# Moving a state-space branch behind the exponentials of an attention loop: one loop from the first rows instead of four stages

## The chip, the cores and the metric

The kernel runs on one core of one Trainium2 chip. The metric is device time in microseconds (us) of that core: the median of the fast runs. In the profile, PE is TensorE (PEld its weight loads), DVE is VectorE, ACT is ScalarE, POOL is GpSimd, SP the engine that issues most transfers. L519 is line 519 of the kernel of that run. The program lists each engine's instructions in a fixed order, with semaphores to wait at. In the traces below, what is listed behind a waiting instruction waits with it: in r8, a VectorE copy out of PSUM whose input was ready began only after the reductions listed before it, the first of which had waited 10.01 us.

## The reference, cut to what matters

```python
x = A_x                                                  # 1 x 2048 x 512, bf16
g = sigmoid((x * gate_w).sum(-1, keepdims=True))
# a: softmax attention, 32 heads of 16, then @ wo
qkv = (x @ wqkv)...; p = softmax(q k^T * 16**-0.5); a = (p v) @ wo
# b: a diagonal state-space model as a long convolution, 512 channels x 128 complex modes
dt = exp(log_dt); K[d,l] = Re sum_n C*exp(dt*A*l)*dt*B
b = causal_conv(x, K) + x * Dskip
return g * a + (1 - g) * b
```

Per head and query row there are 2048 exponentials: 32 x 2048 x 2048 in all, which is 1024 instructions of 128 partitions x 1024 elements on ScalarE. No other engine computes them here.

## The kernel before

It has two blocks with a barrier between them. Block 1 loads, projects (storing Q and K to device memory) and builds powers of the state matrix for 128 time steps with Exp and Sin on ScalarE. Block 2 is the attention loop, with the chunk scan on VectorE and the convolution's matmuls on TensorE placed between the steps, and a closing combine.

```python
# block 1, ScalarE: the tables (64 Exp, 128 Sin of 128x1024)
actc.inc(a.activation(TE[:, u % 8, :], pa_slots[v_re(u) % 2], AF.Exp))          # L435
...
a.activation(TSn[:, u % 2, :], src, AF.Sin)                                      # L442
actc.inc(a.activation(TCs[:, u % 2, :], src, AF.Sin, scale=-1.0, bias=HPI))      # L443
... (cut: projections, products, transfers of the tables through device memory)
# block 2, ScalarE: the softmax exponentials
for c in range(NCHUNK):                                                          # 1024
    a.wait_ge(stc.sem, c + 1)
    ...
    exc.inc(a.activation(ET[:, c % NRCH, 0:QW * n], chunk_src(c)[:, 0:QW * n], AF.Exp, scale=DH ** -0.5))  # L775
# block 2, TensorE
for sx in range(NSTEP):                       # 512 steps of two exponentials
    st_step(sx + LAS)                         # scores, 4 matmuls in 4 row groups    L894
    pv_step(sx)                               # probabilities x V, 4 column groups   L922
    for d in ysched[...]: y_channel(d)        # convolution output, 3 matmuls a channel
# after the loop, VectorE, 16 times
cv2(v.tensor_tensor(fb1, xr, Dbc, ALU.mult)); ... (cut: L872 to L875, gate and add)
```

The softmax here doesn't subtract the row's maximum and nothing guards it: scores larger than these inputs give would overflow.

## Time and profile before

| stretch (us) | what runs | ACT busy | granted clock |
|---|---|---|---|
| 0 to 166 | loads, parameters, projections | 18.6 of 166 | 0.97 |
| 166 to 542 | state-space tables | 203.8 of 376 | 0.50 |
| 542 to 1504 | attention loop | 941.0 of 962 | 0.50 |
| 1504 to 1573 | combine | 0 of 69 | 0.52 |

Median time 1577.24 us (1575.1 to 1579.39, 4 runs).

From the page of the kernel before: busy time of the engines, then busy tenths in 40 slices of the span (a 9 is 90% or more; PEclk is the granted TensorE clock in tenths).

```profile
PE 994.5 (63%) x8332; PEld 294.0 (19%) x8340; DVE 732.8 (47%) x1678; ACT 1163.4 (74%) x1249; POOL 170.6 (11%) x201
...
PE   0199555655653166666566666567888768888744
...
ACT  0100666666662299999899999899999989999920
...
PEclk9999555555555555555555555555555555555555
```

The row ACT shows the stages: nothing, 60%, a gap, then nearly full from slice 14 on, and nothing at the end. The table above is from the view of engine times in four stretches (span, busy time and count for each engine, clock, DMA share, GB/s):

```profile
0.00:166.00 166.00, 86.49 (x347) 34.27 (x354) 118.57 (x194) 18.58 (x23) 1.08 (x9) 0.97 0.42 99
166.00:542.00 376.00, 189.54 (x2296) 82.44 (x2296) 120.56 (x290) 203.83 (x201) 116.53 (x132) 0.50 0.90 193
542.00:1504.00 962.00, 689.88 (x5632) 170.36 (x5628) 434.33 (x1087) 940.95 (x1026) 52.96 (x60) 0.50 0.26 60
1504.00:1573.00 69.00, 28.55 (x62) 6.95 (x64) 59.37 (x108) 0.00 (x0) 0.00 (x0) 0.52 0.19 57
```

And the costliest groups: busy us and mean ns of one, then the idle time of that engine just before them and who ended it.

```profile
L775 ACT ACTIVATE ET<-pr 128x1024 bf16<-128x1024 f32 x1024 | 939.5, 1049 | 48.4 <-PE pr L894 47.7
L922 PE MATMUL pb<-ET,VE 128*32 128x512 bf16 x2048 | 315.7, 607 | 154.5 <-ACT ET L775 154.3
```

So the third stage is bound by ScalarE (one exponential every 939.5 / 1024 = 0.917 us, starts overlapping ends), and the other three stages, 611 us, are not.

### The profile page before, as it was taken

What the parts mean: (1) busy time and instruction counts of PE and PEld (TensorE: products, weight loads), DVE (VectorE), ACT (ScalarE), POOL (GpSimd) and SP (SyncE); (2) the same over time, 40 slices, a digit from 0 to 9 for tenths busy, and PEclk for the clock granted to TensorE, in tenths of its full rate; (3) what the DMA queues carried; (4) which work ended last, traced back from release to release, by engine and by line L of the source; (5) the groups of instructions that cost most, each with busy time, mean ns of one, the idle gap of its engine ahead of it and who ended that gap; (6) DMA issues with size and microseconds to landing.
All of it is one profiled execution on the core that took longest, in us unless ns stands there. A gap on an engine that the chain in (4) does not pass through costs nothing. (4 is left out here: it accounts for less than half of the span.)

```text
span 1572.3 us, 21690 instructions
## 1 busy us (share of the span) xinstructions
PE 994.5 (63%) x8332; PEld 294.0 (19%) x8340; DVE 732.8 (47%) x1678; ACT 1163.4 (74%) x1249; POOL 170.6 (11%) x201
## 2 busy tenths in 40 slices
PE   0199555655653166666566666567888768888744
PEld 0044122222222011111111111111222222222210
DVE  7777233333333248787788782131232123123168
ACT  0100666666662299999899999899999989999920
POOL 0000233333332000000000000000111111111000
PEclk9999555555555555555555555555555555555555
DMA  6513699989999700000100000101555555555312
GB/s 150 54 67 147 137 186 198 205 199 185 206 201 201 181 14 1 1 1 1 54 1 1 1 0 1 49 5 41 121 122 125 134 145 121 128 126 123 88 31 70
DMA packets 346760, 150.21 MB, mean 96 GB/s; under 512 B 320160, under 2 KB 330272, under 8 KB 346656
## 3 DMA queue, kind: packets, MB, share of 16 engines
q1 hardware_dynamic: 331296, 98.47, 29.2%
q0 software_dynamic: 15360, 50.34, 12.9%
q8 instruction: 66, 1.08, 0.3%
q14 instruction: 38, 0.31, 0.1%
HBM read 68.03 MB, written 44.30 MB: 71 GB/s over the span
## 5 line engine op out<-in xcount | busy, mean ns | idle before, releaser
L775 ACT ACTIVATE ET<-pr 128x1024 bf16<-128x1024 f32 x1024 | 939.5, 1049 | 48.4 <-PE pr L894 47.7
L922 PE MATMUL pb<-ET,VE 128*32 128x512 bf16 x2048 | 315.7, 607 | 154.5 <-ACT ET L775 154.3
L894 PE MATMUL pr<-QK 16*128 16x512 bf16 x2048 | 313.5, 603 | 142.6 <-ACT ET L775 89.1
L847 DVE CAST OS<-pb 128x512 bf16<-128x512 f32 x32 | 22.1, 692 | 335.5 <-PE pb L922 335.5
L764 POOL DMA_DIRECT2D Tst<-gm_kp_scr x64 | 56.5, 883 | 920.9 <-PE pb L944 906.9
L397 DVE TENSOR_TENSOR PR<-TE,TCs 128x1024 bf16<-128x1024 bf16 x64 | 44.3, 692 | 237.5 <-ACT TCs L443 119.2
L442 ACT ACTIVATE TSn<-pr 128x1024 bf16<-128x1024 f32 x64 | 65.7, 1026 | 102.6 <-PE pr L488 84.1
L922 PEld LDWEIGHTS pb<-ET,VE 128*32 128x32 bf16 x2048 | 56.5, 101 | 413.1 <-ACT ET L775 411.0
L856 DVE TENSOR_SCALAR ON<-OT,Rz 128x16 bf16<-128x16 bf16 x512 | 121.8, 238 | 18.3
L519 PE MATMUL pb<-urev,Qt 128*128 128x16 bf16 x1024 | 47.2, 192 | 111.8 <-DMA Qt<-gm_pt_scr 72.8
L894 PEld LDWEIGHTS pr<-QK 16*128 16x128 bf16 x2048 | 55.4, 99 | 305.8 <-ACT ET L775 234.1
L273 POOL DMA_DIRECT2D gm_pt_scr<-PR x64 | 56.8, 888 | 371.3 <-DVE PI L398 370.0
L844 DVE CAST Ysb<-pb 128x512 bf16<-128x512 f32 x16 | 11.1, 691 | 159.7 <-PE pb L944 159.6
L435 ACT ACT_TABLE_LOAD x8 | 10.3, 1283 | 100.3 <-PE pr L488 100.3
L940 PE MATMUL pb<-urev,Tst 128*128 128x16 bf16 x512 | 69.9, 193 | 6.2 <-DVE junkb L845 6.2
L488 PE MATMUL pr<-MU,ahl 32*128 32x512 bf16 x128 | 56.1, 608 | 26.0 <-ACT TE L435 22.4
L443 ACT ACTIVATE TCs<-pr,cst 128x1024 bf16<-128x1024 f32 x64 | 71.4, 1115 | 0.0
L488 PE MATMUL pr<-MU,bhl 32*128 32x512 bf16 x128 | 65.8, 616 | 7.8 <-ACT TCs L443 5.8
L435 ACT ACTIVATE TE<-pr 128x1024 bf16<-128x1024 f32 x64 | 62.4, 1022 | 6.8 <-PE pr L488 6.4
L940 PEld LDWEIGHTS pb<-urev,Tst 128*128 128x128 bf16 x512 | 46.3, 104 | 104.2 <-issue 104.2
L944 PE MATMUL pb<-sgi,Pst 128*128 128x15 bf16 x512 | 62.5, 174 | 0.0
L943 PE MATMUL pb<-sgr,Pst 128*128 128x15 bf16 x512 | 62.2, 174 | 0.0
(144 smaller groups left out, 1069.3 us busy)
## 6 DMA issues: line engine op xcount, KB each, us to landing
Pst<-gm_pt_scr SPq DMA_DIRECT2D x64, 512.0 KB, 4.5
gm_pt_scr<-PR POOLq DMA_DIRECT2D x64, 256.0 KB, 4.8
gm_pt_scr<-PI POOLq DMA_DIRECT2D x64, 256.0 KB, 5.3
Tst<-gm_kp_scr POOLq DMA_DIRECT2D x64, 256.0 KB, 5.2
gm_qk_scr<-qkev SPq DMA_DIRECT2D x16, 512.0 KB, 2.6
QK<-gm_qk_scr SPq DMA_DIRECT2D x16, 512.0 KB, 5.6
xr<-in_A_x_dram SPq DMA_DIRECT2D x32, 128.0 KB, 2.1
x_sb<-in_A_x_dram SPq DMA_DIRECT2D x1, 2048.0 KB, 10.9
```

The source lines that it names most:

```text
L273: stq[u % 2].inc(g.dma_start(AP(pt_scr, ((8 * tt) * 2 + part) * NMODE * T, [[T, P], [2 * NMODE * T, 8], [1, T]]), srcb[:, u % 2, :]), 16)
L435: actc.inc(a.activation(TE[:, u % 8, :], pa_slots[v_re(u) % 2], AF.Exp))
L442: a.activation(TSn[:, u % 2, :], src, AF.Sin)
L443: actc.inc(a.activation(TCs[:, u % 2, :], src, AF.Sin, scale=-1.0, bias=HPI))
L488: ins = t.matmul(dstt[:, 512 * bb:512 * (bb + 1)], src[32 * t4:32 * t4 + 32, slot8, :], MU2[32 * t4:32 * t4 + 32, 512 * bprime:512 * (bpri ...
L775: exc.inc(a.activation(ET[:, c % NRCH, 0:QW * n], chunk_src(c)[:, 0:QW * n], AF.Exp, scale=DH ** -0.5))
L856: cv2(v.tensor_scalar(ON[:, c0 + 16 * w:c0 + 16 * w + 16], OT[:, c0:c0 + 16], Rz[:, 4 * i + Bh:4 * i + Bh + 1], None, ALU.mult))
L894: ins = t.matmul(st_dst(tt), QK[32 * j:32 * j + 16, w, 1, 128 * kt:128 * (kt + 1)], QK[32 * j:32 * j + 16, w, 0, QW * qc:QW * (qc + 1)], s ...
L922: ins = t.matmul(half[32 * j:32 * j + 32, :], VE[:, kt, 32 * h:32 * h + 32], ET[:, c % NRCH, QW * (tt % CT):QW * (tt % CT + 1)], start=(kt ...
L940: t.matmul(Yps[:, col:col + NCK], Tst[:, slot, cpos, :], urev[:, :, d], start=True, stop=(NCK == 1))
L943: t.matmul(Yps[:, col + 1:col + NCK], Pst[:, slot, 2 * cpos, :], sgr[:, d, 0:NCK - 1], start=False, stop=False)
L944: ins = t.matmul(Yps[:, col + 1:col + NCK], Pst[:, slot, 2 * cpos + 1, :], sgi[:, d, 0:NCK - 1], start=False, stop=True)
```

## The change

Its intent is to start the 512 attention steps as soon as the first rows and one head group are projected, and to put everything else behind them: the remaining projections, the state-space branch in chunks of 64 steps with its powers made by repeated complex multiplication on VectorE and GpSimd, the scan on GpSimd, and the combine. A small planner in Python walks through the 512 steps. At each step every engine gets a budget in microseconds; side work is a set of generators that say what they wait for and what the next piece will cost. The plan fixes the order of each engine's instructions; the chip then runs them with semaphores.

```diff
+class Sched:
+    def _ok(self, t, req):
+        ... "AFTER": a mark was set so many steps ago; "LOCK": the shared PSUM bank MB is free
+        if self.bud[k] > 0:
+            self.bud[k] -= req[1]
+            return True
+    def step(self, rate):
+        for k, r in rate.items():
+            self.bud[k] = min(self.bud[k] + r, r) if r > 0 else 0.0
+        ... each generator advances while _ok
 ... (cut: buffer placement, automatic semaphores, parameters, tables)
+    def scan():                       # 4 quarters x 31 chunks, on GpSimd
+                e = "POOL"
+                    yield (e, .65)
+                    op(e, ... v.tensor_tensor(s2, G, MU, ALU.mult))     # 128x256 fp32, three more like it
+                yield (e, .35)
+                op(e, ... v.tensor_copy(sg, G))
 ... (cut)
+    for q in range(512):
+        ex(2 * q)
+        if q + 1 < NQ:
+            qk(q + 1)
+        ex(2 * q + 1)
+        rate = dict(PE=.62 if q > 50 else 1.0, DVE=1.5, POOL=1.8)
+        pv(q - 1)                     # (with exceptions at block borders, cut)
+        if kt == 0 and b >= 1:
+            norm(b - 1)
+        if q < len(first):
+            proj(*first[q], mb)
+        sch.step(rate)
```

Nearly all of the side work on TensorE goes through one PSUM bank, MB (a few projections at the start and the last output blocks use others), which VectorE has to copy out before the next user gets it.

## The prediction

> **What bounds it now.** The page's 40 slices and the table of stretches show four stages in series. 0 to 166 us: parameter arithmetic, loads, projections (ScalarE busy 18.6 us). 166 to 542 us: state-space tables, with ScalarE's Exp and Sin, VectorE products and 90% DMA share; ScalarE busy 203.8 of 376 us. 542 to 1504 us: attention, ScalarE busy 941 of 962 us. 1504 to 1573 us: the combine on VectorE, ScalarE idle. So the attention stage is bound by the exponentials: 1024 of 128x1024, one every 0.915 us (group of costliest instructions: 939.5 us busy, plus 48.4 us idle, of which about 20 us lie inside the stage: three reloads of Q and K and the start). In that stage TensorE is 690 of 962 us busy at a granted clock of 0.50, waiting mostly for ET; VectorE is under half busy. About 610 us run outside the ScalarE-bound stage.
>
> **What the change does.** It leaves the number and shape of exponentials, 1024 of 128x1024, so the floor is 1024 x 0.917 = 939 us. All ScalarE state-space work (128 Sin, 64 Exp, 200 us) is gone: powers come from VectorE and GpSimd multiplications. Projections, tables, scan and the closing combine become side work put behind the attention steps (two exponentials, 1.83 us each step).
>
> Does it fit in 512 steps (about 940 us)?
> - TensorE: two groups of four 512-column matmuls take 0.61 us each (timeline), 1.2 us per step, leaving 0.6. Side work, estimated from traced rates (0.38 to 0.41 us per 512-column matmul; 44 ns extra per small one): projections 75, kernel and state stages 80, output stage 75 to 100, output projection 25: about 260 us against 300 free. It fits, but tightly.
> - VectorE: about 400 us plus 32 normalizations (4 instructions instead of 22), against 940. Fits.
> - GpSimd: about 124 scan steps of five small instructions. The trace has no GpSimd arithmetic. The Trainium skill, "GPSIMD Engine Reference", section 3.1, gives 4497 ns for a 2048-element fp32 tensor_tensor; scaled to 256 elements with its fixed part that is about 0.7 us, so my estimate is about 400 us for the scan, 500 in all. No trace here shows it.
>
> **Critical path after.** Head: transposed load of x (2.5 us landing per 128 KB), weights (Wv took 9.6 us), first projections, decay Exp/Sin: about 20 us to the first exponential. The first 15 steps carry a projection each: some 12 us extra. Then 940 us. Tail: last normalization, four output blocks, about 12 us. Sum 985. In-order queues let a late VectorE eviction, transfer or scan step block TensorE and so ScalarE; I add 40 us for stalls, about 0.08 us per step.
>
> **Prediction: 1025 us**, 80% range 975 to 1115. Faster by over 2%: 0.97; within 2%: 0.01; slower: 0.02.
>
> **What would show it.** Right: ScalarE over 90% busy, its first 128x1024 exponential before 30 us, mean duration still about 1050 ns, no Sin besides one head pair, DMA traffic well below 150 MB, GpSimd over 400 us busy and never the releaser of long ScalarE waits, nothing but a few output blocks after the last exponential. TensorE 80 to 95% busy in the steady stretches, clock mostly 0.5. Wrong: ScalarE idle summing well above 60 us between exponentials, released by matmuls that themselves waited for GpSimd (scan) or for VectorE (evictions of the one shared PSUM bank); or a long tail.
>
> **What would make it wrong.** GpSimd instructions 30% over the estimate, or slowed by VectorE sharing its memory port, would stretch the scan and hold TensorE in order: 50 to 150 us. TensorE bursts over 1.83 us a step lose ScalarE time for good. A higher granted clock from the denser matmul stream would bring it down to about 980 us.

## The result

The change takes 1262.16 us median (1256.71 to 1263.3, 4 runs): 0.7996 of the time before, 95% interval 0.7977 to 0.8015. (Ratios are the mean time of a kernel's fast runs over that of the kernel before's fast runs of the same rounds, so not quite the quotient of the medians.) It is clearly faster, and 237 us slower than predicted.

The page after, the same rows, with GpSimd added:

```profile
PE 818.9 (65%) x6378; PEld 247.3 (20%) x6400; DVE 664.4 (53%) x958; ACT 967.4 (77%) x1032; POOL 622.4 (49%) x704
...
ACT  5545666987988667677669988479679778999995
POOL 3799770000009888889830000899999984000000
PEclk9867656755555555555555555555555555557855
```

Lay the rows ACT and POOL over each other. ScalarE is mostly at 40 to 70% where GpSimd is busy, and at 80% or more in most slices where GpSimd rests. The view of stretches says it in numbers (fourth bracket ACT, fifth POOL):

```profile
0.00:240.00 240.00, 138.67 (x786) 32.50 (x800) 184.38 (x209) 149.85 (x160) 144.57 (x77) 0.73 0.32 73
240.00:400.00 160.00, 105.91 (x920) 26.03 (x916) 98.06 (x212) 135.57 (x148) 21.79 (x29) 0.50 0.63 158
400.00:640.00 240.00, 118.94 (x1000) 27.79 (x996) 197.43 (x265) 164.07 (x177) 209.97 (x273) 0.52 0.29 82
640.00:800.00 160.00, 125.70 (x1096) 47.95 (x1096) 40.62 (x73) 132.24 (x140) 10.69 (x15) 0.50 0.48 118
800.00:1050.00 250.00, 178.16 (x1477) 68.54 (x1477) 105.10 (x122) 195.50 (x206) 228.60 (x308) 0.50 0.31 74
1050.00:1262.00 212.00, 151.57 (x1115) 44.49 (x1121) 38.84 (x81) 190.18 (x204) 6.77 (x6) 0.60 0.13 34
```

In the first, third and fifth stretch, where GpSimd is 60 to 91% busy, ScalarE idles 90, 76 and 54 us: 220 of its 294 idle us (18 of the first 90 are the head, before the first exponential). The groups of instructions:

```profile
L519 ACT ACTIVATE ET<-SC 128x1024 bf16<-128x1024 f32 x1024 | 960.9, 1067 | 263.9 <-PE SC L426 230.7 <-PE OA L426 19.8
L842 POOL TENSOR_TENSOR s_143<-G,MI 128x256 f32<-128x256 f32 x120 | 104.1, 868 | 0.0
```

The exponentials cost what they did. What is new is 263.9 us of idling before them (48.4 before), ended mostly by a score matmul (230.7 us of it). But TensorE was waiting too. Here is how, from the order of time at 36 us (start, duration, engine, instruction; in brackets the idle time before it and who ended it):

```profile
35.91 1.22 DVE L544 TENSOR_TENSOR pt_114<-L_108 128x1024 f32<-128x1024 f32 x1
...
37.61 8.26 POOL L942 COPY UB<-X_146 64x2048 bf16<-64x2048 bf16 x2 [25.25 <-DMA X_146<-gm_xrd]
37.74 4.62 DVE L544 TENSOR_TENSOR pt_115<-L_108 128x1024 f32<-128x1024 f32 x1
...
42.28 0.68 DVE L488 CAST VE<-MB 128x512 bf16<-128x512 f32 x1
...
43.11 1.02 PE L426 MATMUL MB<-xT,Wk 128*128 128x512 bf16 x4 [3.54 <-DVE VE L488]
...
44.50 1.94 ACT L519 ACTIVATE ET<-SC 128x1024 bf16<-128x1024 f32 x2 [3.27 <-PE SC L426]
```

A VectorE product that took 1.22 us at 35.9 takes 4.62 us at 37.7, when GpSimd has just begun two copies of 3.66 and 4.48 us. It ends at 42.36 us, 1.09 us after the first copy; the next two-input product (42.89 to 46.43, 0.69 us undisturbed) ends 0.55 us after the second. So each seems to have stood still while the copy ran. The PSUM copy listed behind it on VectorE comes late, so the next projection on TensorE waits 3.54 us for bank MB, so the score matmuls listed behind that come late, and ScalarE idles 3.27 us. Time that ScalarE loses is never made up.

The same stretching is there for every VectorE product with two sources in SBUF that both stretches contain, and for some instructions with one source, but for none that reads PSUM. From the groups of instructions of VectorE, first at 240 to 360 us (GpSimd idle), then at 400 to 640 us (GpSimd scanning); the mean ns of one is the number after the comma:

```profile
L544 DVE TENSOR_TENSOR PT<-tt_133,tt_134 128x512 bf16<-128x512 bf16 x38 | 16.1, 425 | 1.3
L757 DVE CAST Sst<-MB 128x512 bf16<-128x512 f32 x20 | 13.8, 690 | 24.0 <-DMA gm_sd<-Sst 13.6 <-PE MB L426 10.4
L539 DVE STREAM_TRANSPOSE OnT_57<-ON 128x512 bf16<-128x512 bf16 x2 | 1.4, 711 | 0.1
L502 DVE TENSOR_SCALAR Qm<-Q_50,msk 128x512 bf16<-128x512 bf16 x3 | 1.0, 346 | 0.0
...
L544 DVE TENSOR_TENSOR PT<-tt_133,tt_134 128x512 bf16<-128x512 bf16 x42 | 30.2, 719 | 1.4
L757 DVE CAST Sst<-MB 128x512 bf16<-128x512 f32 x25 | 17.2, 688 | 15.6 <-PE MB L426 15.6
L502 DVE TENSOR_SCALAR Qm<-Q_51,msk 128x512 bf16<-128x512 bf16 x6 | 3.7, 615 | 0.0
L539 DVE STREAM_TRANSPOSE OnT_58<-ON 128x512 bf16<-128x512 bf16 x3 | 2.1, 712 | 0.1
```

425 ns became 719; the copy out of PSUM kept 690. Of the instructions with one SBUF source (the mask that TENSOR_SCALAR multiplies by is one number a partition), TENSOR_SCALAR went from 346 to 615 ns, while the transposition of ON (711, 712) and the reciprocal (253, 254) kept their time. GpSimd suffers as well: the four groups of 128x256 products of its scan have medians of 731 to 738 ns and maxima of 1187 to 1261. The Trainium skill says why, in "SBUF — State Buffer", section "SBUF: two separate sides": GpSimd and VectorE share one port pair to SBUF, which is an exclusive lock and not a split of bandwidth. A VectorE instruction in a two-port mode, or with two SBUF inputs while GpSimd's reads SBUF, competes for it with a GpSimd instruction; whichever starts first holds it for its whole length, and the other fully blocks. The numbers above agree with it, down to the instructions that are not stretched; in which mode the one-source instructions ran, the trace does not show.

A second path is in the same trace. VectorE also waits for GpSimd to finish: the weighting of the next states (SW) waited 99.7 us until the scan had moved on (its copies into SG end the waits), and the page puts 18% of the chain that ended last on GpSimd. Its lines:

```profile
L800 DVE TENSOR_TENSOR SW<-SG_140,WR 128x512 f32<-128x512 bf16 (+1 forms) x32 | 33.2, 1076 | 65.2 <-POOL SG_140 L851 54.7
L800 DVE TENSOR_TENSOR SW<-SG_139,WR 128x512 f32<-128x512 bf16 (+1 forms) x32 | 29.6, 965 | 64.3 <-POOL SG_139 L851 45.0
```

Moving the scan to VectorE removes both paths together; r3 below isolates the first.

### The profile page after: what moved, and what is told of

It is laid out like the page before. It is cut to its first block, busy times and chain, and to the rows that moved or that the text cites. A ratio compares the mean times of both kernels' runs of the same rounds, so it can differ in the third digit from the quotient of the medians.

```text
span 1261.5 us, 16332 instructions
## 1 busy us (share of the span) xinstructions
PE 818.9 (65%) x6378; PEld 247.3 (20%) x6400; DVE 664.4 (53%) x958; ACT 967.4 (77%) x1032; POOL 622.4 (49%) x704
## 4 chain that ended last, share of the span: by engine, by line
DVE 36%; POOL 18%; PE 18%; ACT 17%; DMA 5%; issue 3%; SPq 2%; ACTq 0%; DVEq 0%; POOLq 0%
ACT ET L519 17%; PE MB L426 8%; PE SC L426 5%; DVE SW L800 4%; PE OA L426 4%; DVE sw_145 L805 4%; POOL s_142 L839 4%; POOL G L848 4%; POOL s_142 L845 4%; DVE tt_133 L544 4%; DVE tt_134 L544 4%; DVE PT L544 3%; POOL s_143 L842 3%; DMA gm_sd<-Sst 2%; DVE pt_115 L544 2%
## 5 line engine op out<-in xcount | busy, mean ns | idle before, releaser
L519 ACT ACTIVATE ET<-SC 128x1024 bf16<-128x1024 f32 x1024 | 960.9, 1067 | 263.9 <-PE SC L426 230.7
L426 PE MATMUL SC<-Qm,KT 32*128 32x512 bf16 x2048 | 300.0, 576 | 181.1 <-ACT ET L519 165.8
L426 PE MATMUL OA<-ET,VE 128*32 128x512 bf16 x2048 | 296.6, 583 | 23.4 <-DVE OT L534 22.2
L426 PEld LDWEIGHTS SC<-Qm,KT 32*128 32x128 bf16 x2048 | 55.2, 98 | 372.3 <-ACT ET L519 323.6
L842 POOL TENSOR_TENSOR s_143<-G,MI 128x256 f32<-128x256 f32 x120 | 104.1, 868 | 0.0
L845 POOL TENSOR_TENSOR s_142<-s_142,SW 128x256 f32<-128x256 f32 x120 | 103.5, 862 | 0.0
L848 POOL TENSOR_TENSOR G<-s_142,s_143 128x256 f32<-128x256 f32 x120 | 97.2, 810 | 9.3
L839 POOL TENSOR_TENSOR s_142<-G,MU 128x256 f32<-128x256 f32 x120 | 101.5, 845 | 0.0
L426 PE MATMUL MB<-Tt,Uy 128*64 128x64 bf16 x256 | 66.9, 261 | 31.3 <-DVE Yst L905 30.6
L800 DVE TENSOR_TENSOR SW<-SG_140,WR 128x512 f32<-128x512 bf16 (+1 forms) x32 | 33.2, 1076 | 65.2 <-POOL SG_140 L851 54.7
L800 DVE TENSOR_TENSOR SW<-SG_139,WR 128x512 f32<-128x512 bf16 (+1 forms) x32 | 29.6, 965 | 64.3 <-POOL SG_139 L851 45.0
L426 PE MATMUL MB<-Py,SG_140 128*32 128x64 bf16 x512 | 46.4, 271 | 8.6 <-POOL SG_140 L851 8.6
```

The costliest lines, as they stand in the source:

```text
L426: op("PE", lambda t: t.matmul(out(), lhsT(), rhs(), start=start, stop=stop, skip_group_check=True, **kw), R, W)
L519: op("ACT", lambda a: a.activation(ET(1024 * e, [[1, 1024]]), sc(0, [[1, 1024]]), AF.Exp, scale=DH ** -0.5), [(sc, 0, h // 2), (sc, 1, h / ...
L800: op("DVE", lambda v, so=so, o=o, nc_=nc_, ri=ri: v.tensor_tensor(SW(o + 128 * ri, [[256, nc_], [1, 128]]), sg(so + 128 * ri, [[256, nc_], ...
L839: op(e, lambda v: v.tensor_tensor(s2(0, [[128, 2], [1, 128]]), G(0, [[128, 2], [1, 128]]), MU(d0, [[0, 2], [1, 128]]), ALU.mult), key("G", ...
L842: op(e, lambda v: v.tensor_tensor(s3(0, [[128, 2], [1, 128]]), G(128, [[-128, 2], [1, 128]]), MI(d0, [[D, 2], [1, 128]]), ALU.mult), key(" ...
L845: op(e, lambda v, o=o: v.tensor_tensor(s2(0, [[1, 256]]), s2(0, [[1, 256]]), SW(o, [[1, 256]]), ALU.add), [(s2, 0)] + swk, [(s2, 0)])
```

## The experiments

Theories, as they were named in the expectations. A: GpSimd and VectorE hold each other up over SBUF, VectorE reaches its PSUM copies late, TensorE waits in order, ScalarE idles. B: TensorE bursts at half clock, and the single bank, are the limit. C: VectorE is simply overloaded. D: the plan's prices are too low, so the chip lags behind it. All kernels ran 3 rounds beside the kernel before; "idle" is the idle time just before the 1024 exponentials.

| run | median us | of before | idle us | result |
|---|---|---|---|---|
| the change | 1262.2 | 0.7996 | 263.9 | correct |
| r1 scan on VectorE | 1164.6 | 0.7393 | 144.0 | correct |
| r2 all on VectorE | 1143.1 | 0.7254 | 117.3 | correct |
| r3 r2 + unconnected GpSimd work | 1311.4 | 0.8327 | 282.4 | correct |
| r4 prices raised | 1194.3 | 0.7582 | 157.6 | correct |
| r5 attention alone | 994.7 | 0.6317 | 13.3 | wrong |
| r6 output stage reordered | 1263.5 | 0.8028 | 255.1 | correct |
| r7 r2 + spacing, 1.70 us a step | 1093.1 | 0.6943 | 71.8 | correct |
| r8 r7 + reordered output | 1084.2 | 0.6887 | 55.3 | correct |
| r9 r8 + transfers spaced | 1035.9 | 0.6573 | 26.4 | correct |
| r10 r5 + unconnected GpSimd work | 995.3 | 0.6318 | 14.4 | wrong |
| r11 r2 at 1.70 us a step | 1144.1 | 0.7262 | 141.6 | correct |
| r12 GpSimd kept, plan repaired | 1157.5 | 0.7348 | 119.3 | correct |

### r1: the scan on VectorE

```diff
-                e = "POOL"
+                e = "DVE"            # each product .43 instead of .65, copy .3 instead of .35
+    sch.add(scan(), low=True)        # planned after all other work of a step
```

> The scan (about 600 small instructions, 440 us busy on GpSimd in the changed kernel) runs on VectorE instead, planned at 0.43 us an instruction and last in priority. Theory A (GpSimd and VectorE hold each other up when both use SBUF; VectorE then reaches its PSUM copies late, TensorE waits in order, ScalarE idles): GpSimd is idle after about 230 us, VectorE table products take 0.42 us throughout (0.72 while the scan ran), ScalarE idle after 240 us falls from about 155 us to under 60; the first 240 us stay as slow as they were (idle about 95 us). Time 1150 to 1190 us. Rival B (TensorE bursts at half clock and the single shared PSUM bank are what stalls): TensorE has the same work, so within 2% of 1262 us. Rival C (VectorE now simply overloaded): slower than 1262.

Measured 1164.6 us: 98 us less, although VectorE now does 768 us of work instead of 664. B and C fall as main causes, since TensorE has the same matmuls and VectorE has more to do. Between exponentials after 240 us ScalarE idles 72 us instead of 191; under 60 was expected. Before 240 us, where the bases and copies still run on GpSimd and the scan has not begun in either kernel, it idles 72 us against 73.

### r2: all arithmetic of the loop on VectorE

```diff
+ (as r1, and:)
-            yield from base(qr, "POOL", 1, .0022)
+            yield from base(qr, "DVE", 1, .00105)
- u copies and skip product: op("POOL", ...)
+ u copies and skip product: op("DVE", ...)
-        rate = dict(..., DVE=1.5, POOL=1.8)
+        rate = dict(..., DVE=1.60, POOL=1.8)
```

> All GpSimd arithmetic of the loop (scan, bases, u copies, skip product) runs on VectorE; VectorE plan 1.60 us a step. A: 128x1024 fp32 products keep 1.22 us (up to 4.6 before), ScalarE idle in all falls from about 267 us between instructions to under 110; time 1070 to 1120 us. B: within 2% of 1262. C: VectorE over 90% busy and slower than r1.

Measured 1143.1 us. The direction is A's, the size was missed by 23 us. The 128x1024 fp32 products are back at 1.22 us. Two new losses took part of the gain: VectorE, in order, waited 7 to 9 us at a time for the transfer that its copy of u reads (ScalarE idled 7.0, 6.3 and 7.9 us there), and about 45 us of work was left after the last exponential.

### r3: GpSimd work that nobody needs

```diff
+ (r2, and in each step from 16 to 495, twice:)
+   op("POOL", lambda g: g.tensor_tensor(z1, z0, z0, ALU.mult), [z0], [z1])   # 128x256 fp32
```

> As r2, plus 960 GpSimd multiplications of 128x256 fp32 on a scratch buffer of their own, which nothing waits for and which wait for nothing. A: VectorE instructions with SBUF sources are stretched again wherever GpSimd runs, PSUM copies keep 0.69 us, and the time rises well over r2: 1180 to 1350 us. If contention is harmless (the loss came from waiting for the results of GpSimd), it stays within 2% of r2.

Measured 1311.4 us, 168 us over r2, by instructions that have no connection with the rest. The groups of r2, then of r3:

```profile
L544 DVE TENSOR_TENSOR PT<-tt,tt 128x512 bf16<-128x512 bf16 x96 | 40.8, 425 | 3.3
L757 DVE CAST Sst<-MB 128x512 bf16<-128x512 f32 x64 | 44.1, 689 | 57.3 <-DMA gm_sd<-Sst 30.9 <-PE MB L426 26.4
```

```profile
L1088 POOL TENSOR_TENSOR z<-z 128x256 f32<-128x256 f32 x960 | 721.5, 752 | 75.0
L546 DVE TENSOR_TENSOR PT<-tt,tt 128x512 bf16<-128x512 bf16 x96 | 58.4, 608 | 3.3
L759 DVE CAST Sst<-MB 128x512 bf16<-128x512 f32 x64 | 44.0, 687 | 57.5 <-DMA gm_sd<-Sst 31.4
```

The product goes from 425 to 608 ns on average, the PSUM copy stays. VectorE is busy 980 us instead of 756 with the same instructions. Contention alone, without anyone waiting for GpSimd's results, costs ScalarE 165 us of idling. This shows A's mechanism: it is enough for a loss of this size. How the changed kernel's own loss divides between contention and waits for the scan was not measured.

### r10: the control

```diff
+ (r5, attention alone, with the same 960 GpSimd instructions)
```

> r5 (attention alone) plus the same 960 unconnected GpSimd multiplications as r3. VectorE has little SBUF work here (135 us busy of 993, most of it copies out of PSUM) and slack. A: ScalarE and TensorE are not touched by GpSimd, so within 1.5% of r5 (995 us); if GpSimd work by itself slowed ScalarE, TensorE or the transfers, clearly over 1020.

Measured 995.3 us against 994.7 without them. GpSimd work does not slow ScalarE or TensorE by itself. This run moves only 12 MB, so transfers are better judged in r3, which moves the same 107 MB as r2: VectorE waited for the rows of u 26.3 us in both, and for the states' transfers 31.4 us against 30.9. So the cost of r3 comes through VectorE.

### r5: attention alone

```diff
-    for th in (projs(), params(), base(...), table(), weigh(), scan(), ystage(), ublocks(), gate(), combine(), outs()):
+    for th in (projs(), gate(), combine(), outs()):      # and combine without the convolution's output
```

> The changed kernel with its state-space branch cut out (tables, weighting, scan, state and output stages; a wrong result on purpose); projections, gate, attention and output projection stay where they are, SBUF is not shared between buffers. The prediction's sum without its stall allowance, 985 us, was meant to hold even with the state-space work behind it. If that sum is right, 975 to 1000 us. If the head, the 15 projection steps and the loop are slower by themselves, over 1020.

Measured 994.7 us. The prediction's sum for head, loop and tail (985) holds within 1%. So what was missed comes from putting the state-space work behind the loop.

### r4: the same engines, honest prices

```diff
-                    yield (e, .65)
+                    yield (e, .9)          # copy .35 -> .55, u copy 3.0 -> 4.3, base .0022 -> .0026,
+                                           # weighting 1.2 and 1.15 -> 2.2 and 1.9 (VectorE)
```

> The engines of the changed kernel are kept; only the prices in its plan are set nearer to what the trace shows (scan instruction 0.9 instead of 0.65, copy 0.55 instead of 0.35, u copy 4.3 instead of 3.0, base 18% up, weighting 2.2 and 1.9 instead of 1.2 and 1.15), so less work is placed in each step and the plan ends at step 514 instead of 481. If a plan that lags behind is the whole loss (theory D): 1120 to 1170 us. A: the instructions are as slow as before but are waited for less; 1190 to 1250 us.

Measured 1194.3 us, 68 us less than the change with the same instructions on the same engines. The result lies in A's range, near its bottom, and above D's. Prices are a real part of the loss: idle time falls from 263.9 to 157.6 us although every engine keeps its work, so where the plan asks for less in a step, a late engine has time to catch up. Part of that gain goes into a longer tail (53 us from the last exponential's start to the end, in the change 14), since this plan ends later.

### r6: the output stage in another order

```diff
- for each channel: real, then imaginary part   (neighbours in the same column group)
+ for four channels: real parts, then imaginary parts (neighbours in different column groups)
+ price in the plan: .25 us for two channels instead of .3
```

> The changed kernel with one thing altered: in the output stage the 32-column matmuls are issued real part of four channels, then imaginary part of four channels, so that neighbours lie in different column groups (now two neighbours accumulate in the same group), at 0.25 us a channel pair in the plan instead of 0.3. Rival B (TensorE bursts): the stage now costs 0.47 us a channel pair against 0.3 planned; if that matters, 40 to 70 us are saved (1190 to 1220 us). A: the stage fills only 300 of 1262 us and ScalarE idles mostly elsewhere; 1225 to 1255.

Measured 1263.5 us: no change, so less gain than even A's guess of 7 to 37 us. Yet the edit did what it was for, as its page shows:

```profile
PE 768.9 (61%) x6378; PEld 215.0 (17%) x6400; DVE 673.9 (53%) x958; ACT 974.9 (77%) x1032; POOL 627.9 (50%) x704
```

TensorE is busy 768.9 us instead of 818.9. Fifty microseconds of TensorE time were worth nothing here. The bursts of B fall as a cause for the changed kernel; its other half, the single bank, is not touched by this edit and comes back in r7.

### r11 and r7: pace, and spacing

```diff
+ r11: r2 with DVE=1.70 in the budget, nothing else
+ r7:  r11, and
+      bank MB goes to the next user only in a later step than the one that freed it
+      the copies of u are planned 8 steps after their transfer was issued
```

> r2 with VectorE at 1.70 us a step and nothing else, to separate the three changes of r7. The shorter tail (plan of the last output stages ends about 25 steps earlier) gives 10 to 25 us: 1115 to 1135 us; the spacing then accounts for the other 25 to 40 us of r7.

> r2 with three changes of the plan and no other engine for any work: the shared PSUM bank is handed to the next user only in a later step, the copies of u are placed 8 steps after their transfer was issued, and VectorE gets 1.70 us of work a step so that the plan ends earlier. In r2 ScalarE idled 33 us at 120 to 200 us behind VectorE waiting for that transfer, and some 45 us at 250 to 600 us where two state matmul groups in one step waited for each other's eviction. If these two waits are the rest of the stalls: 1065 to 1105 us. If VectorE is now too full: 1120 to 1160.

r11 measured 1144.1 us: nothing gained, and the expectation of 10 to 25 us was wrong. The tail did get shorter (the last exponential starts at 1121.9 of 1141.6 us, in r2 at 1095.4 of 1141.5), but the loop gave all of it back: idle 141.6 instead of 117.3 us. r7 measured 1093.1 us, so the two spacings give 51 us together; how they share it was not separated. In r2 two groups of state matmuls stood in one step, and TensorE sat out the copies of bank MB between them (1.44 and 0.86 us at 405 to 407 us), so the single bank of B does cost time, once GpSimd is cleared.

### r8 and r9: the output order again, and all transfers

```diff
+ r8: r7 with the output order of r6
+ r9: r8, and
-            yield ("AFTER", f"sg{...}", 3)          # loaded states
+            yield ("AFTER", f"sg{...}", 8)
+            gate rows: 6 steps after their transfer; skip rows: 5; the gate's Exp 12 steps after its input
```

> r7 plus the reordered output stage of r6. 15 to 40 us under r7, 1040 to 1080 us, since in r2 ScalarE idled some 35 us in the stretches where TensorE was over 90% busy with that stage.

> r8 plus more steps between a transfer and its first use on VectorE (gate rows 6, skip rows 5, loaded states 8 instead of 3), and the gate's Exp 12 steps after its input. In r8 ScalarE idled 10.7 and 16.7 us behind gate rows, 9.6 us behind loaded states and 7.7 us behind skip rows, all of them VectorE waiting in order for a transfer. If that is the rest: 1035 to 1055 us. If moving work later only shifts the waits: within 1% of r8 (1084).

r8 measured 1084.2 us: 9 us, less than the 15 to 40 expected. Its order of time showed the next chain. The lines are a transfer issue, a VectorE reduction, a TensorE projection, an exponential:

```profile
113.33 16.44 SPq L960 DMA_DIRECT2D xg<-in_A_x_dram  x8
...
120.41 0.69 DVE L962 CUSTOM_DVE_ANT_0 gj<-xg,gw 128x512 bf16<-128x512 bf16 x1 [10.01 <-DMA xg<-in_A_x_dram]
...
125.89 1.06 PE L428 MATMUL MB<-xT,Wk 128*128 128x512 bf16 x2 [11.04 <-DVE KT L494]
...
127.53 2.85 ACT L521 ACTIVATE ET<-SC 128x1024 bf16<-128x1024 f32 x3 [10.71 <-PE SC L428]
```

VectorE waits 10 us for rows of the gate, which is first multiplied in at 1000 us, and ScalarE pays 10.7 us. With the use planned later, r9 measured 1035.9 us (1035.1 to 1036.1), correct: 0.6573 of the kernel before, and 0.6573 / 0.7996 = 0.82 of the change. It beats both. Its page:

```profile
PE 756.8 (73%) x6400; PEld 214.9 (21%) x6400; DVE 766.3 (74%) x1650; ACT 971.4 (94%) x1032; POOL 14.0 (1%) x12
...
ACT  4899999989899999999999999999999999999990
...
L521 ACT ACTIVATE ET<-SC 128x1024 bf16<-128x1024 f32 x1024 | 965.0, 1116 | 26.4 <-PE SC L428 25.5
```

### r12: the repairs of the plan with GpSimd kept

```diff
+ the change, with scan products at .8, copies .5, u copy 4.3, base .0026, weighting 1.7 and 1.6,
+ bank and transfers spaced, output reordered; scan, bases and u copies stay on GpSimd,
+ the skip product goes to VectorE; VectorE's budget stays 1.5 us a step (r9: 1.70)
```

> The scan, bases and u copies stay on GpSimd, but with all repairs of the plan: prices nearer to the trace (scan instruction 0.8), spaced bank and transfers, reordered output stage. If the plan was the whole loss, it reaches r9 or r8 (1040 to 1090 us). A: VectorE and GpSimd still stretch each other, so 1110 to 1170 us, clearly over r8.

Measured 1157.5 us. With all repairs the plan still leaves 122 us to r9, with idle time 119.3 against 26.4 us. Some 27 us of the 122 are a longer tail (53 us from the last exponential's start to the end, in r9 26), since this plan also ends later. The rest goes with the work kept on GpSimd: contention, and 103 us in which VectorE's weighting waits for the scan, which were not separated. So this better plan is not enough. Yet the two repairs overlap: clearing GpSimd alone leaves 117.3 us of idle time (r2), repairing the plan alone 119.3, both together 26.4, from 263.9.

## Why the prediction was wrong

- **What bounds the kernel before, and the floor**: right. The exponentials are the same (mean 1067 against 1049 ns), the first one starts at 17.8 us (predicted about 20), and 14 us lie between the start of the last one and the end (predicted a tail of about 12). Attention alone takes 994.7 us (the sum said 985).
- **The step that failed** is this one: "I add 40 us for stalls, about 0.08 us per step". The changed kernel has 1262 - 995 = 267 us over attention alone, where 40 were allowed. In the order in which the experiments took it away: 119 us by clearing GpSimd (r2), 50 by the pace and by spacing the bank and the u copies (r7), 9 by the output order (r8), 48 by spacing the transfers (r9); 41 remain. These shares depend on the order: prices alone, with GpSimd kept, gave 68 (r4), and all repairs with GpSimd kept gave 105 (r12). That r9 ends near the predicted 1025 us is no support for the prediction: the program had to be repaired four times to get there.
- **The mechanism was named as a risk, not counted.** "GpSimd instructions 30% over the estimate, or slowed by VectorE sharing its memory port, would stretch the scan": the scan's products had a median of 0.731 us, as estimated (0.7), but a mean of 0.81 to 0.87; GpSimd was busy 622 us, not 500. The effect that r3 isolates runs the other way and was not in the text: VectorE is slowed by GpSimd, 0.425 to 0.719 us for a table product, and VectorE owns the copies that TensorE waits for. VectorE ("about 400 us ... against 940. Fits.") and GpSimd ("500 in all") were each added up as if the other were idle. Even the 150 us at the top of the named risk would not have covered the 267.
- **Average load was taken for fit.** TensorE, VectorE and GpSimd were all well under full (65, 53, 49% busy). r6 shows how little the sum means here: 50 us less TensorE work, no gain. What counts is whether each instruction in an ordered queue is ready when its turn comes.
- **Side work on TensorE**: 818.9 - 300.0 - 296.6 = 222 us busy against 260 estimated. The output stage alone was 66.9 + 46.4 + 46.4 = 160 us instead of 75 to 100; by r6 this did not matter.
- **Signs named in advance**: DMA traffic 107 MB (well below 150), clock mostly 0.5, short tail, GpSimd over 400 us: as said. ScalarE over 90% busy: no, 77%. "ScalarE idle summing well above 60 us": yes, 264, so the prediction's own test pointed to the right failure. TensorE 80 to 95% busy: no, 65% over the span.

What stays open: why an exponential in the stretches with the output stage starts only about every 1.0 us instead of 0.92 while ScalarE counts as fully busy (in r9 at 640 to 680 us, 40 starts in 40 us); how the two spacings of r7 share their 51 us; and how much of the changed kernel's loss is contention and how much is waiting for the scan.

## What to carry to other kernels

When work is hidden behind a bound engine, budget the engines pairwise, not one by one: GpSimd arithmetic was not free here while VectorE worked in SBUF, and it reached the bound engine because VectorE also empties PSUM for the engine that feeds the bound one. In fixed in-order queues, put many steps between the issue of a transfer and its first use and between two users of one bank, because one early wait for something that is not urgent held up everything listed behind it (r8). To find such losses, follow one idle gap of the bound engine back through the order of time, then delete or duplicate the suspected work without touching any dependence.

## What the Trainium skill lacked or had wrong

- "SBUF — State Buffer", section "SBUF: two separate sides": the exclusive lock between VectorE and GpSimd is there and the runs agree, but no time for two streams of ordinary products (further on, the page has two ratios, without their operations or sizes). Here: 425 to 719 ns for a 128x512 bf16 product on VectorE; 0.73 (median) to 1.26 us (longest) for a 128x256 fp32 product on GpSimd; 1.22 to 4.62 us for a 128x1024 fp32 product on VectorE beside a GpSimd copy; PSUM copies unchanged at 0.69 us; for the whole kernel 168 us from 960 unconnected GpSimd products (r3).
- "GPSIMD Engine Reference", section 3.1, times a tensor_tensor only at 2048 elements (4497 ns). Scaling gave 0.7 us for 256; the median in the scan was 0.731 us (0.612 for a square of one source in r10, where VectorE works little in SBUF). Section 4.1 calls one-input work "roughly line-rate"; the strided copy of 64x2048 bf16 took 3.64 to 4.48 us on GpSimd, beside VectorE's work, and 1.89 us on VectorE (r2, median). How much of that is contention was not measured.
- "TensorE: Matmul & The Clock Gate", section "Why this matters for your kernels", advises against idle gaps over about 3 us. In the kernel before, at 900 to 960 us, no gap between matmuls was longer than 0.30 us and TensorE was 67% busy, and the granted clock stayed at 0.50; in r9, at the same times, TensorE was 88% busy with gaps up to 1.22 us, at 0.51. So in these runs short gaps alone did not bring the full clock. This does not contradict the advice, which is about not losing the clock; what share of busy time brings it back was not measured.
- No page of the skill was found to say what the experiments turned on most: that side work has to be planned with slack, since one early wait in an ordered queue is passed on to the bound engine in full (10.0 us of VectorE waiting became 10.7 us of ScalarE idling in r8).
